# Linear attention and a gated MLP on one core: query features of the last two batches without the maximum, their two sums weighted afterwards, and a new order table

## The chip, the cores and the metric

The kernel runs on one core of a Trainium2 chip. The metric is the device time of one execution in microseconds (us). The time before is 264.87 us, the median of three runs that lie between 264.82 and 264.91 us.

The engines are named as the profile names them: PE (matrix products and transposes), PEld (its weight loads), DVE (vector), ACT (scalar, exponentials), POOL (GpSimd, which also issues the loads that change type) and SP (which issues most other transfers).

## The reference

There are 8 batches, 8 heads, 576 tokens, 64 numbers a head and 128 features. All inputs and the output are float32.

```python
def phi(x):
    proj = np.einsum('bhsd,df->bhsf', x, w_phi)
    proj = proj - np.max(np.abs(proj), axis=-1, keepdims=True)
    return np.concatenate([np.exp(proj), np.exp(-proj)], axis=-1)
q_p, k_p = phi(q), phi(k)
kv = einsum('bhsf,bhsd->bhfd', k_p, v);  z = sum(k_p, axis=2)
attn = (q_p @ kv) / (q_p . z + 1e-6)          # then heads side by side: x, 512 wide
h = max(x @ w_in, 0);  u, v = halves of h     # 1024 wide
v_n = (v - mean) / sqrt(var + 1e-6)
v_s = einsum('ts,bsd->btd', w_spatial, v_n) + b_spatial
out = (u * v_s) @ w_out
```

Each token and head has a maximum m over its projections p. The first half of its features is exp(p - m), the second exp(-p + m).

## The kernel before

**Tiling.** The 576 tokens of a batch are 4 blocks of 128 and a tail of 64. The tails of two batches make one tile, a group g (groups 0 to 3). Query work is cut into units (b, cc, hg): a batch, two of its four token blocks, four of its eight heads, so four units a batch, and one unit for each group of tails.

**A unit of queries before.** `qp` projects the queries with the tokens on the partitions (`by_token`, L578, 8 products of 64 rows). `qm` takes the largest absolute value over the features on DVE (`maxima`, L583). `qs` splits it on POOL into a high and a low bfloat16 part, mhl (`split`, L678 and L679). `qt` turns mhl on PE (`max_t`, L683), and `qc` copies it to mT (L277 on ACT or L279 on DVE). `qf` projects again with the features on the partitions and takes the maximum away inside the product: `features` issues 2 products with wphi (L689) and 8 with sel, a matrix of minus ones (L693). Two `qe` take the exponentials on ACT (L698), for p and for -p. `qn` (L748) sums over both halves of the features into one pair of PSUM banks, 16 products that accumulate in twos; column 64 of each head is the denominator. `qr` takes its reciprocal (L754) and `qx` multiplies (L759); both are on DVE and write x. The tails do the same with `qpt` to `qxt` (L799, L804, L809).

**Behind it.** The blocks of x are turned, by a DMA (`xx`) or on PE (`tx`, L824, copied by `txc`). `vm` and `um` are products with the halves of w_in (L853, L921), `vr` and `ur` their positive parts. `vb` and `va` are the moments on DVE (L875, L879), `vw` the root on POOL (L858 to L860), `vn` the normalised v on POOL (L863), `sm` the spatial product (L935, L937), `sg` the gate on DVE (L944), `om` the last product (L950), `oc` its copy, `od` its store. The second letter or a final t marks tails (`omt`, `sgt`).

**Keys.** `kp`, `km`, `ke` and `kem` make the key features; there the maximum is not subtracted. It goes as exp(-m) and exp(m) onto v instead: `vs` on POOL (L633), `vst` for tails (L645). `kv` is the sum over the tokens (L663, L665).

**What sets the order.** Nothing is scheduled by the program: ORDER is a table of words, and each word issues one step. `qn.7.0.0:2,3` is step qn of unit (7, 0, 0) with banks 2 and 3; `qx.7.0.0:0@V` runs on DVE (A is ACT, P is POOL, S is SP) into buffer 0 of its kind. Each engine works its own list in this order, and waits where an input or a buffer is not ready. `warm.5:3` issues 5 products of ident with itself that nobody reads (L365), into bank 3. BUFS gives the number of buffers of a kind.

**Loads.** Batch 0 of q and k is loaded as float32 by `lkf` and `lqf` from SP and ACT into buffers that are free at the start, and turned on PE as float32 (`turn`, L509). From batch 1 on, POOL issues loads that change the type to bfloat16 (`lk` L398, `lq` L402); these are turned on PE for batches 1 and, in part, 2, and by DMA later. Two steps for loading batch 1 as float32 (`lkg`, `lqg`) are in the program but not in the table.

**Ends.** The table ends with `om.6.3`, its copy on ACT and its store from SP. `omh`, `och` and `odh` do a block of the output in two halves of its columns.

Of the kernel before, what the change touches and what calls it, by code (L numbers as in the profile page):

```python
# [17 lines left out]
cident@P lkf.2:0@S lkf.1:4@A cident2@P warm.27:0 lkt.0:0@S lkf.0:1@A zsp@P zmhl.0@P lphi@S csel@P lqf.1:0@S zvst.0@P  # L18
lqf.0:1@S lkf.3:2@S tk.0.1.0:3 warm.3:0 chalf@P lv.0.0:3@S csel2@P warm.5:4 warm.3:0 lqt.0:1@S tkc.0.1.0:5@A lq.1:0@P
tk.0.0.0:2 warm.6:0 ctab@A lk.1:1@P tk.0.0.1:3 warm.12:0 tkc.0.0.0:0@V tkc.0.0.1@A cphi@V zvnt.0@P lvt.0:0@S  # L20
kp.0.0:4,5 kp.0.2:6,7 km.0.0:0@V warm.5:3 ke.0.2.1:0@A warm.5:2 warm.5:0 lv.0.1:1@S zmhl.3@P warm.5:2 ckt.0:0@P
ke.0.2.0@A warm.5:1 zmhl.2@P tkt.0:2 tq.0.1.0:3 kem.0.0:0@A km.0.2:1@V ke.0.0.0:1@A tq.0.1.1:1 warm.10:0 lkt.1:0@S
vsz.0.0:0@P zmhl.1@P tqc.0.1.0:6@A tktc.0:0@V kp.0.1:6,7 tqc.0.1.1@V warm.5:2 ke.0.1.0:2@A warm.5:0 warm.5:2 warm.5:0
ke.0.0.1@A km.0.1@V qp.0.0.1:2,3 warm.5:0 tq.0.0.1:1 qm.0.0.1:0@V kpt.0:4,5 warm.10:0 kem.0.1@A tqc.0.0.1:2@A
ke.0.1.1@A qp.0.1.1:0,1 lv.1.0:2@S qs.0.0.1:2@P tq.1.0.0:2 qm.0.1.1:1@V tq.0.0.0:3 kem.0.2:1@A tq.1.1.1:6 tqc.0.0.0@A
tk.0.1.1:7 tqc.1.0.0:1@V ket.0.0:0@A warm.5:0 qs.0.1.1:1@P tkc.0.1.1@V tq.1.1.0:3 warm.6:1 tqc.1.1.1:4@V vsz.0.1:1@A
qt.0.1.1:7 warm.5:2 ket.0.1@A tqc.1.1.0@V vs.0.1.1@P qt.0.0.1:6 qp.0.1.0:0,1 qc.0.0.1:0@V lbs:2@S kp.0.3:2,3
qm.0.1.0:2@V warm.5:6 qc.0.1.1:1@A vs.0.0.1@P ke.0.3.0:3@A warm.5:7 warm.5:6 kmt.0:0@V tq.1.0.1:6 ke.0.3.1@A
qs.0.1.0:2@P tk.1.1.0:7 lsp:0@P tk.1.1.1:0 tk.1.0.1:1 warm.4:4 tkc.1.1.1:3@A tkc.1.1.0@V lspt:3@P km.0.3@V
tkc.1.0.1:0@A lv.1.1:0@S qt.0.1.0:7 warm.5:4 lq.2:0@P cqt.0:0@A warm.5:4 kp.1.1:0,1 kemt.0:0@A vs.0.1.0@P tqc.1.0.1@A  # L30
tqt.0:5 km.1.1:2@V tk.1.0.0:4 tqtc.0:0@A warm.5:2 warm.4:3 lk.2:1@P tkc.1.0.0@A qpt.0:2,3 qc.0.1.0:3@V ke.1.1.0:4@A
# [135 lines left out]
def kernel(  # L167
# [900 lines left out]
```

## Time and profile before

| what | us |
| --- | --- |
| median of three runs | 264.87 |
| the profiled execution | 264.64 |
| its span, first to last instruction | 262.8 |
| outside the span | 1.84 |
| busy in the span: PE, DVE, ACT, POOL | 250.8, 206.6, 202.2, 185.1 |

A row of a timeline gives the start, the length and the engine, then the line, the operation, what is written and read, and a count of instructions that are alike. Products on PE overlap: one takes 0.2 to 0.4 us from its start to its end, but the next may start long before. What a row costs PE is therefore the distance from its start to the start of the next row. The busy sums count the fillers of `warm` too. Granted clock is the share of full speed that PE was given; it is 1.00 in every stretch of 10 us.

### The profile page before, as it was taken

The page shows a single profiled execution, that of the slowest core. Times are in us where ns is not written, and L with a number is a line of the kernel's source. Part 1 is how long each engine was busy: PE and PEld are TensorE (multiplying, and loading weights), DVE is VectorE, ACT ScalarE, POOL GpSimd, SP SyncE. Part 2 cuts the span into 40 slices and gives each one's busy share as a digit, 9 for nine tenths or more (in the row PEclk, how much of TensorE's full clock was granted, in tenths as well). Part 3 has the DMA queues.
Part 4 walks back from the last instruction along what each step waited for, and adds up shares of the span by engine and source line. Part 5 has one row for each costly group of instructions (what it writes and reads, how often), then busy time and mean ns, then how long its engine had stood idle before and what let it go on. Part 6 is the DMA issues. An engine that isn't in the chain of part 4 may idle for free.

```text
span 262.8 us, 8513 instructions
## 1 busy us (share of the span) xinstructions
PE 250.8 (95%) x3464; PEld 164.0 (62%) x3499; DVE 206.6 (79%) x362; ACT 202.2 (77%) x330; POOL 185.1 (70%) x338
## 2 busy tenths in 40 slices
PE   7999989999999998989999999999999999999993
PEld 7978768666566565666665766555547586446441
DVE  0679889998899898798899877999987848655730
ACT  3689989999769999999999896997899762453032
POOL 8627996999997996687999992369989820288000
PEclk9999999999999999999999999999999999999999
DMA  7999999962797979998999999998630130044045
GB/s 196 305 193 296 192 203 230 234 75 42 198 209 164 193 123 141 209 143 87 208 205 197 225 107 144 212 197 209 178 127 2 40 84 8 36 159 162 11 148 203
DMA packets 80090, 41.35 MB, mean 157 GB/s; under 512 B 48946, under 2 KB 75442, under 8 KB 80052
## 3 DMA queue, kind: packets, MB, share of 16 engines
q1 hardware_dynamic: 58628, 29.93, 53.1%
q0 software_dynamic: 20592, 10.10, 33.2%
q10 hardware_dynamic: 832, 0.79, 0.9%
q8 instruction: 27, 0.44, 0.7%
q14 instruction: 11, 0.09, 0.1%
HBM read 32.82 MB, written 9.44 MB: 161 GB/s over the span
## 4 chain that ended last, share of the span: by engine, by line
PE 67%; POOL 19%; DVE 5%; DMA 4%; issue 3%; ACT 0%; POOLq 0%; DVEq 0%; ACTq 0%
PE banks L853 10%; PE banks L950 9%; PE banks L935 9%; PE banks L921 8%; POOL vs L633 5%; PE banks L748 5%; PE banks L578 4%; PE banks L663 4%; DMA ld<-in_q_dram 4%; DVE mq L583 3%; PE banks L689 3%; POOL vn L863 2%; POOL vst L645 2%; PE banks L937 2%; PE banks L693 2%
## 5 line engine op out<-in xcount | busy, mean ns | idle before, releaser
L698 ACT ACTIVATE qf<-banks 128x1024 bf16<-128x1024 f32 x72 | 70.1, 1030 | 6.0 <-PE banks L693 5.5
L587 ACT ACTIVATE kf<-banks 128x1024 bf16<-128x1024 f32 x64 | 63.9, 1037 | 5.2 <-PE banks L578 4.8
L633 POOL TENSOR_TENSOR vs<-v,em 128x512 bf16<-128x512 f32 x64 | 65.7, 1043 | 3.0 <-ACT em L592 2.8
L583 DVE TENSOR_REDUCE mq<-banks 128x8 f32<-128x1024 f32 x36 | 43.4, 1220 | 4.1 <-PE banks L578 2.5
L583 DVE TENSOR_REDUCE mk<-banks 128x8 f32<-128x1024 f32 x32 | 38.8, 1218 | 4.5 <-ACT kf L587 2.4
L921 PE MATMUL banks<-xT,w_u 128*128 128x512 bf16 x128 | 32.3, 380 | 0.0
L935 PE MATMUL banks<-w_spT,vn 128*128 128x512 bf16 x116 | 31.6, 379 | 0.7 <-issue 0.2
L853 PE MATMUL banks<-w_v,xT 128*128 128x512 bf16 x118 | 31.2, 379 | 0.5
L950 PE MATMUL banks<-w_out,uT 128*128 128x512 bf16 x113 | 29.6, 379 | 0.7 <-issue 0.2
L277 ACT COPY ob<-banks 128x512 f32<-128x512 f32 x23 | 13.5, 597 | 19.4 <-PE banks L950 18.7
L944 DVE TENSOR_TENSOR uT<-banks,uT 128x512 bf16<-128x512 f32 x32 | 21.4, 683 | 6.4 <-PE banks L937 6.1
L863 POOL TENSOR_SCALAR vn<-vr,mv,rs 128x512 bf16<-128x512 bf16 x32 | 24.4, 767 | 1.2
L663 PEld LDWEIGHTS <-kf 128*128 128x128 bf16 x512 | 21.9, 97 | 4.3 <-issue 0.8
L663 PE MATMUL banks<-vs,kf 128*128 128x66 bf16 x512 | 23.9, 194 | 0.5 <-POOL vs L633 0.3
L875 DVE BATCH_NORM_STATS2 st<-vr 128x6 f32<-128x512 bf16 x32 | 21.5, 683 | 3.5 <-ACT vr L283 3.2
L578 PE MATMUL banks<-wphi,T 64*128 64x128 bf16 x512 | 22.8, 217 | 0.4
L759 DVE TENSOR_TENSOR x<-banks,rc 128x512 bf16<-128x512 f32 x32 | 22.1, 690 | 0.9
L283 ACT ACTIVATE vr<-banks 128x512 bf16<-128x512 f32 (+1 forms) x28 | 16.8, 606 | 7.3 <-PE banks L853 5.8
L748 PEld LDWEIGHTS <-qf 128*128 128x128 bf16 x512 | 19.2, 98 | 4.4 <-issue 0.9
L365 PE MATMUL banks<-ident 128*128 128x128 bf16 x237 | 19.4, 234 | 2.1 <-POOL ident L279 1.7
L665 PE MATMUL banks<-vst,kft 128*128 128x66 bf16 x128 | 21.1, 191 | 0.1
L748 PE MATMUL banks<-kv,qf 128*128 128x66 bf16 x512 | 21.0, 193 | 0.0
(123 smaller groups left out, 481.2 us busy)
## 6 DMA issues: line engine op xcount, KB each, us to landing
v<-in_v_dram SPq DMA_DIRECT2D x16, 512.0 KB, 6.9
out_dram<-ob SPq DMA_DIRECT2D x31, 256.0 KB, 3.0
ld<-in_q_dram POOLq DMA_DIRECT2D x7, 512.0 KB, 10.8
ld<-in_k_dram POOLq DMA_DIRECT2D x7, 512.0 KB, 10.4
uT<-in_q_dram SPq DMA_DIRECT2D x2, 512.0 KB, 5.3
vt<-in_v_dram SPq DMA_DIRECT2D x8, 128.0 KB, 8.6
out_dram<-ob SPq DMA_DIRECT2D x8, 128.0 KB, 3.3
vn<-in_moe_w_spatial_dram POOLq DMA_DIRECT2D x1, 576.0 KB, 7.8
```

Source lines behind the costliest of these rows:

```text
L578: nc.tensor.matmul(out=bank(banks[y])[:, n * F:(n + 1) * F], lhsT=xT[halves[y], n, :], rhs=wphi[halves[y], :], start=True, stop=True)
L583: nc.vector.tensor_reduce(out=out_, in_=pp.rearrange("p y (n f) -> p y n f", f=F), axis=AX.X, op=ALU.max, apply_absolute_value=True)
L587: nc.scalar.activation(out=kf[:, s].rearrange("p y n f -> p y (n f)"), in_=pp, func=AF.Exp, bias=0.0, scale=(1.0, -1.0)[s])
L633: ENG[e].tensor_tensor(out=get("vs", (b, j))[:, s, :, 0:D], in0=at["v", (b, j // 2)][:, (j % 2) * n:(j % 2 + 1) * n, :], in1=at["em", (b, ...
L663: nc.tensor.matmul(out=pv[:, hh, s, :], lhsT=kf[:, s, c % 2, 2 * hh + c // 2, :], rhs=w[:, s, NB * hh + c, :], start=(c == 0), stop=False)
L698: nc.scalar.activation(out=at["qf", u][:, s].rearrange("p y n t -> p y (n t)"), in_=at["pq", u], func=AF.Exp, bias=0.0, scale=(1.0, -1.0)[s])
L748: nc.tensor.matmul(out=at["pn", u][:, y, n, :], lhsT=f[:, s, y, n, :], rhs=at["kv", b][:, hg * HH + n, s, :], start=(s == 0), stop=(s == 1))
L853: nc.tensor.matmul(out=bank(place)[r], lhsT=lhs[:, kc, r], rhs=w_v[:, kc, :], start=(kc == 0), stop=(kc == KC - 1))
L863: ENG[e].tensor_scalar(out=out_, in0=in_, scalar1=mv, scalar2=rs, op0=ALU.add, op1=ALU.mult)
L921: nc.tensor.matmul(out=bank(place).rearrange("p (c t) -> p c t", c=NB), lhsT=w_u[:, kc, dc * P:(dc + 1) * P], rhs=at["xT", b][:, :, kc, :] ...
L935: nc.tensor.matmul(out=bank(place), lhsT=at["vn", b][:, c, cs], rhs=w_spT[:, c, 0:T0], start=(c == 0), stop=False)
L950: nc.tensor.matmul(out=bank(place), lhsT=at["uT", b][:, dc, c * P:(c + 1) * P], rhs=w_out[:, dc, :], start=(dc == 0), stop=(dc == KC - 1))
```

## The change

The units of batches 6 and 7 and the tail unit of group 3 no longer subtract the maximum from the query projections, in the way the keys do already. With f1 = exp(p) and f2 = exp(-p), the result is (exp(-m) f1.kv1 + exp(m) f2.kv2) divided by the same of z. It may be multiplied above and below by exp(-m), so only the first sum needs a weight, w = exp(-2m).

- `qw` (ACT) makes w from the maximum; `qs`, `qt` and `qc` go.
- `qg` is the projection alone, the 2 products with wphi; the 8 with sel go.
- `qn` becomes `qna` and `qnb`, 8 products each, for the two halves of the features, each into its own pair of banks.
- `qy` (DVE) writes w times the first sum to tq, 528 float32 numbers a partition; `qz` (DVE) adds the second sum; `qv` (DVE) takes the reciprocal of the denominators. `qu` multiplies tq by it into x and runs on POOL. `qr` and `qx` go.
- tq has one buffer, wq has six. The float32 copy of w_phi now lies in a buffer of x.

The table is new from its first word. Beside these steps it loads batch 1 of q and k by `lkg` and `lqg` (float32, issued by SP) and no longer by POOL; the 8 turnings of batch 1 are float32 with it. Ahead of the last product stand 195 fillers in place of 232, and behind it 10 in place of 5. It ends with `om.7.2` and the second half of `omh.7.3`. Many copies and positive parts go to another engine of ACT and DVE than before.

```diff
-BUFS = dict(ld=3, ..., mq=4, mhl=4, mT=4,
+BUFS = dict(ld=3, ..., mq=4, mhl=4, mT=4, wq=6, tq=1,
...
+        wq=([P, 2, HH], FP32),
+        tq=([P, 2, HH, DA], FP32),
...
-    wphi_f = const("wphi_f", [D, F], FP32)
+    wphi_f = buf["x"][0][0:D].rearrange("p a h d -> p (a h d)").bitcast(FP32)[:, 0:F]
...
+    def features_u(u, xT):
+        banks = [places.pop(0), places.pop(0)]
+        for y in range(2):
+            nc.tensor.matmul(out=bank(banks[y]).rearrange("p (n t) -> p n t", n=HH), lhsT=wphi[halves[y], :],
+                             rhs=xT[halves[y]], start=True, stop=True)
+        at["pq", u] = pair(*banks)
+
+    def weight(u):
+        nc.scalar.activation(out=get("wq", u), in_=at["mq", u], func=AF.Exp, bias=0.0, scale=-2.0)
...
+    def half_sums(b, cc, hg, s):
+        u = (b, cc, hg)
+        f = at["qf", u]
+        pn = at["pn", u, s] = sums((places.pop(0), places.pop(0)))
+        for y in range(2):
+            for n in range(HH):
+                nc.tensor.matmul(out=pn[:, y, n, :], lhsT=f[:, s, y, n, :], rhs=at["kv", b][:, hg * HH + n, s, :],
+                                 start=True, stop=True)
...
+    def weigh(u, w, r=slice(0, P)):
+        nc.vector.tensor_tensor(out=get("tq", u)[r], in0=at["pn", u, 0][r],
+                                in1=at["wq", w][r].unsqueeze(3).to_broadcast([r.stop - r.start, 2, HH, DA]), op=ALU.mult)
+
+    def join(u, r=slice(0, P)):
+        t = at["tq", u][r]
+        nc.vector.tensor_tensor(out=t, in0=at["pn", u, 1][r], in1=t, op=ALU.add)
+
+    def inverse(u, r=slice(0, P)):
+        nc.vector.reciprocal(out=get("rc", u)[r], in_=at["tq", u][r, :, :, D:D + 1])
+
+    def divide(e, out_, u, r=slice(0, P)):
+        ENG[e].tensor_tensor(out=out_, in0=at["tq", u][r, :, :, 0:D],
+                             in1=at["rc", u][r].to_broadcast([r.stop - r.start, 2, HH, D]), op=ALU.mult)
```

The tails do the same by `qwt`, `qgt`, `qnat`, `qnbt`, `qyt`, `qzt`, `qvt`, `qut`. One line of the old table and one of the new, both from the end of batch 7:

```diff
-qn.7.1.1:4,5 qx.7.0.0:1@V vr.6.3:0@A txt.3.2:2 um.6.3:3 qr.7.1.1:1@V sg.5.1@V qx.7.1.1:2@V vm.6.0:1 txtc.3.2:0@V
+qz.7.1.1@V tx.7.1:1 txc.7.0:0@A om.5.0:7 qv.7.1.1:2@V vb.6.1:3@V qu.7.1.1:2@P umt.3:0 txc.7.1@V vb.6.3:1@V
```

Three places show what moves. The first is PE in batch 7. Before, from the last subtraction of one unit through the next unit's two products with wphi to its first subtraction:

```order
L693 LDWEIGHTS sel
L693 MATMUL banks<-mT_114,sel 128x128
L689 LDWEIGHTS wphi
L689 MATMUL banks<-T_68,wphi 128x512
L689 LDWEIGHTS wphi
L689 MATMUL banks<-T_68,wphi 128x512
L693 LDWEIGHTS sel
L693 MATMUL banks<-mT_113,sel 128x128
```

After, the projection of unit (7, 1, 0), between the second sums of two other units (L703 is the product of `features_u`, L789 that of `half_sums`):

```order
L789 LDWEIGHTS qf_127
L789 MATMUL banks<-kv_102,qf_127 128x66
L703 LDWEIGHTS wphi
L703 MATMUL banks<-T_68,wphi 128x512
L703 LDWEIGHTS wphi
L703 MATMUL banks<-T_68,wphi 128x512
L789 LDWEIGHTS qf_126
L789 MATMUL banks<-kv_103,qf_126 128x66
```

The projection stands alone; the subtractions that followed it are gone, and other units' sums stand around it.

The second place is DVE at the last two units of batch 7, whose results are turned on PE next. Before, each is a reciprocal and a product straight into x:

```order
L754 RECIPROCAL rc_122<-banks 128x8
L759 TENSOR_TENSOR x_127<-banks,rc_122 128x2x256
L754 RECIPROCAL rc_124<-banks 128x8
L759 TENSOR_TENSOR x_126<-banks,rc_124 128x2x256
L875 BN_STATS st_139<-vr_134 128x6
```

After (L801 weighs, L806 adds, L809 inverts; L985 and L989 are the moments of batch 6, L282 copies):

```order
L801 TENSOR_TENSOR tq_123<-banks,wq_117 128x528
L989 BN_AGGR mv_154<-st_146 128x2
L806 TENSOR_TENSOR tq_123<-banks,tq_123 128x528
L809 RECIPROCAL rc_131<-tq_123 128x8
L985 BN_STATS st_149<-vr_141 128x6
L282 COPY xT_136<-banks 128x512
L985 BN_STATS st_147<-vr_144 128x6
L989 BN_AGGR mv_153<-st_147 128x2
L801 TENSOR_TENSOR tq_123<-banks,wq_121 128x528
L989 BN_AGGR mv_154<-st_149 128x2
L806 TENSOR_TENSOR tq_123<-banks,tq_123 128x528
L809 RECIPROCAL rc_129<-tq_123 128x8
```

Each unit has three DVE steps instead of two, x is no longer written by DVE, and the moments of batch 6 stand between the units. Both units write the one buffer tq_123.

The third place is POOL at the same units. Before, no unit's result passes POOL; there stand only the moments' root and the normalisation of batch 6 (L858 to L863):

```order
L858 TENSOR_SCALAR mv_144<-mv_144 128x2
L859 TENSOR_SCALAR mv_144<-mv_144 128x2
L860 TENSOR_TENSOR rs_150<-mv_144,neghalf 128x2
L863 TENSOR_SCALAR vn_154<-vr_138,mv_144,rs_150 128x512
L858 TENSOR_SCALAR mv_143<-mv_143 128x2
```

After, the division of the last two units (L812) stands ahead of and behind that work (L968 to L973):

```order
L812 TENSOR_TENSOR x_134<-tq_123,rc_131 128x2x256
L968 TENSOR_SCALAR mv_154<-mv_154 128x2
L969 TENSOR_SCALAR mv_154<-mv_154 128x2
L970 TENSOR_TENSOR rs_160<-mv_154,neghalf 128x2
L973 TENSOR_SCALAR vn_163<-vr_143,mv_154,rs_160 128x512
L812 TENSOR_TENSOR x_134<-tq_123,rc_129 128x2x256
L968 TENSOR_SCALAR mv_153<-mv_153 128x2
```

The last unit's division waits on POOL behind a root and a normalisation, and the next weighing on DVE may write tq only when the division before it has read it.

More of the change, by code (lines that the diff above doesn't have):

```diff
@@ L28 @@
[L28 to L31, printed above, removed]
-warm.5:6 qmt.0:3@V warm.5:5 vstz.0:0@P qp.0.0.0:6,7 vst.0.0.1@P qf.0.1.0:4,5 ke.1.1.1@A lqt.1:1@S qm.0.0.0:0@V
@@ L159 @@
+od.6.3@S om.7.0:3 oc.7.1:3@A od.7.1@S omh.7.3.0:0 oc.7.0:2@V om.7.2:2 och.7.3.0:0@A od.7.0@S odh.7.3.0@A omh.7.3.1
+oc.7.2:4@V warm.5:7 och.7.3.1@A warm.5:5 od.7.2@S odh.7.3.1@A
 """
-BUFS = dict(ld=3, T=7, v=4, tl=1, tf=2, tT=1, vt=1, kf=5, kft=1, mk=4, mkt=1, em=4, emt=1, vs=4, vst=1, kv=3, mq=4, mhl=4, mT=4,
+BUFS = dict(ld=3, T=7, v=4, tl=1, tf=2, tT=1, vt=1, kf=5, kft=1, mk=4, mkt=1, em=4, emt=1, vs=4, vst=1, kv=3, mq=4, mhl=4, mT=4, wq=6, tq=1,
             qf=5, rc=3, x=3, xt=1, xT=3, xTt=2, vr=5, st=4, mv=6, rs=5, vn=3, vnt=2, uT=3, uTt=2, ob=5)
```

330 lines of the change are left out of this document (195 added, 135 removed).

## Prediction

> **What bounds the kernel now.** I read the page first, then the stretches of 10 us, then the chain that ended last, then PE's timeline near the end. The page gives each engine's busy time:
>
> ```profile
> PE 250.8 (95%) x3464; PEld 164.0 (62%) x3499; DVE 206.6 (79%) x362; ACT 202.2 (77%) x330; POOL 185.1 (70%) x338
> ...
> PE 67%; POOL 19%; DVE 5%; DMA 4%; issue 3%; ACT 0%; POOLq 0%; DVEq 0%; ACTq 0%
> ```
>
> The second row is the share of each engine in the chain. PE holds two thirds of it, and POOL a fifth. Where, the stretches say (start:end, length, then busy time of PE, PEld, DVE, ACT and POOL with their counts, granted clock, DMA share, GB/s):
>
> ```profile
> 100.00:110.00 10.00, 9.26 (x147) 6.26 (x146) 7.89 (x16) 9.34 (x14) 5.36 (x8) 1.00 1.29 194
> 110.00:120.00 10.00, 8.98 (x155) 6.10 (x155) 9.46 (x17) 8.94 (x18) 8.65 (x17) 1.00 1.00 139
> ...
> 210.00:220.00 10.00, 9.79 (x211) 7.54 (x212) 5.56 (x14) 5.94 (x11) 1.57 (x2) 1.00 0.26 56
> 182.00:215.00 33.00, 32.58 (x509) 20.92 (x515) 26.10 (x48) 26.78 (x44) 27.04 (x49) 1.00 0.32 92
> ```
>
> Between 100 and 120 us PE stands for 0.74 + 1.02 = 1.76 us. From 182 us on it has next to no idle time (0.42 of 33 us), while DVE falls to 5.56 and POOL to 1.57 of 10 us. The edited units lie in this last regime: there a product less on PE is time won, and work added to DVE and POOL has room. The head, in which PE waits for loads and is fed with fillers, has rows of its own below.
>
> **What the nine units lose on PE.** Rows of PE's timeline; the distance between starts is the cost:
>
> ```profile
> 205.39 0.38 PE L689 MATMUL banks<-T,wphi 64*128 64x512 bf16 x2
> 205.60 0.39 PE L693 MATMUL banks<-mT,sel 64*128 64x128 bf16 x8
> 205.83 0.38 PE L689 MATMUL banks<-T,wphi 64*128 64x512 bf16 x2
> 206.04 0.39 PE L693 MATMUL banks<-mT,sel 64*128 64x128 bf16 x8
> 206.36 1.04 PE L1017 MATMUL banks<-w_out,uTt 128*128 128x512 bf16 x4
> ...
> 208.31 0.67 PE L748 MATMUL banks<-kv,qf 128*128 128x66 bf16 x16
> 208.83 0.27 PE L683 MATMUL banks<-ident,mhl 128*128 128x128 bf16 x2
> 208.94 1.03 PE L935 MATMUL banks<-w_spT,vn 128*128 128x512 bf16 x3
> ```
>
> The 8 subtractions take 205.83 - 205.60 = 0.23 us, and 2.07 over eight units and one tail. A turn of the maximum takes half of 208.94 - 208.83, 0.055 us, so 0.50 over nine. Together **-2.57 us**, all on the path by the rows above. The sums stay 16 products (0.52 us), only in two banks more. Going from products of 64 rows to 128 costs 206.36 - 206.04 - 0.23 = 0.09 us more; the new table has 53 runs of 64-row work where the old had 55. At 0.09 us out and, by estimate, as much in, that is 0.2 to 0.4: **-0.3**.
>
> **The head.** The table's fillers ahead of the last product go from 232 to 195. Batch 1 is turned as float32. The rows of fillers, of float32 turnings and of a bfloat16 one between them:
>
> ```profile
> 7.09 0.50 PE L365 MATMUL banks<-ident 128*128 128x128 bf16 x6
> 7.43 0.61 PE L509 MATMUL banks<-ident_f,ob 128*128 128x128 f32 x4
> 7.87 0.83 PE L365 MATMUL banks<-ident 128*128 128x128 bf16 x12
> ...
> 17.30 0.40 PE L509 MATMUL banks<-ident,ld 128*128 128x128 bf16 x4 [0.60 <-DMA ld<-in_q_dram]
> 17.54 0.61 PE L509 MATMUL banks<-ident_f,uT 128*128 128x128 f32 x4
> ```
>
> A filler takes (7.43 - 7.09)/6 = 0.057 us, so 37 fewer are 2.1 us. They are not work but cover for waits; taking them out wins only what the waits themselves lose. A float32 turning takes 7.87 - 7.43 = 0.44 against 17.54 - 17.30 = 0.24, so eight cost 0.20 each, 1.6 us, in a part where PE has room. If the waits shrink as the fillers do, the head is worth 1.6 - 2.1 = **-0.5 us**. Bounds: nothing of the fillers comes back (+1.6, float32 turnings exposed) and all of it with the turnings hidden (-2.1). I take the middle since PE's work in the head is about the fillers that go.
>
> The Trainium skill (FP8 and Floating Point Precision, TensorE Precision Notes) says that true FP32 makes four passes through the array. The trace does not bear that out for these turnings: 0.44 against 0.24 is not two passes. What four would do stands among the rivals.
>
> What makes this possible is how the loads stand:
>
> ```profile
> 6.50 10.76 DMA ld<-in_q_dram
> ...
> ld<-in_q_dram POOLq DMA_DIRECT2D x7, 512.0 KB, 10.8
> ...
> uT<-in_q_dram SPq DMA_DIRECT2D x2, 512.0 KB, 5.3
> ...
> 3.37 1.14 SPq L386 DMA_DIRECT2D uT<-in_q_dram  x2
> ```
>
> Batch 1's queries sit on the chain for 10.76 us. Issued by SP as float32, loads of that kind landed after 5.3 us, not 10.8. SP pays 1.14/2 = 0.57 us an issue, 2.3 us for four, and the loads of v and of the tails behind them start that much later.
>
> **What DVE, ACT and POOL gain.** Groups that do what the new steps do (count, busy time, mean ns of one):
>
> ```profile
> L759 DVE TENSOR_TENSOR x<-banks,rc 128x512 bf16<-128x512 f32 x32 | 22.1, 690 | 0.9
> L944 DVE TENSOR_TENSOR uT<-banks,uT 128x512 bf16<-128x512 f32 x32 | 21.4, 683 | 6.4 <-PE banks L937 6.1
> L279 DVE COPY ob<-banks 128x512 f32<-128x512 f32 x12 | 8.1, 677 | 0.1
> L633 POOL TENSOR_TENSOR vs<-v,em 128x512 bf16<-128x512 f32 x64 | 65.7, 1043 | 3.0 <-ACT em L592 2.8
> L863 POOL TENSOR_SCALAR vn<-vr,mv,rs 128x512 bf16<-128x512 bf16 x32 | 24.4, 767 | 1.2
> L860 POOL TENSOR_TENSOR rs<-mv,neghalf 128x2 f32<-128x2 f32 x16 | 11.2, 699 | 0.0
> L754 DVE RECIPROCAL rc<-banks 128x8 f32<-128x8 f32 x32 | 6.5, 203 | 5.2 <-PE banks L748 3.1 <-PE banks L683 1.4 <-PE banks L365 0.4
> L592 ACT ACTIVATE em<-mk 128x8 f32<-128x8 f32 x8 | 1.2, 206 | 0.4 <-DVE mk L583 0.4
> 227.84 0.19 POOL L858 TENSOR_SCALAR mv<-mv 128x2 f32<-128x2 f32 x1 [16.27 <-DVE mv L879]
> ```
>
> Weighing and adding read PSUM and one SBUF tile; the nearest rows are 690 and 683 ns, and writing float32 costs nothing extra (677 for the copy to ob). For 528 in place of 512 numbers I take 0.71 us each; bounds are 0.68 and, if the float32 operand from SBUF is as dear as on POOL, 1.04. DVE gains 9 x (2 x 0.71 - 0.69) = 6.6 us less some copies of mT. POOL's division is nearest to vs, float32 by a broadcast into bfloat16: 1.04 us, 9.4 in all, less the splits; the 16.27 us for which POOL stood idle before 227.84 are about where it goes. The weight is 0.21 us on ACT. None of it is on the path by load.
>
> By latency it can be. A unit is now weigh, add, invert, divide, 0.71 + 0.71 + 0.20 + 1.04 = 2.66 us, where reciprocal and product took 0.89; and tq has one buffer, so DVE may not weigh the next unit before POOL has divided this one. I walked the new order by these durations against PE's work between. Two places are tight. At `tx.7.0` the tail's division (POOL) holds tq, the unit's weighing starts after it, and x comes some 0.4 to 0.5 us after PE is ready. At `tx.7.2` the last division stands on POOL behind a root (0.19 + 0.19 + 0.70) and a normalisation (0.77), and x comes about when PE does: 0 to 0.5. For both I take **+0.8 us**.
>
> **The end.** Rows of the last copy, and the stores by queue:
>
> ```profile
> 257.62 0.59 ACT L277 COPY ob<-banks 128x512 f32<-128x512 f32 x1 [0.66 <-PE banks L950]
> 258.21 0.44 PE L365 MATMUL banks<-ident 128*128 128x128 bf16 x5
> 258.45 0.59 ACT L277 COPY ob<-banks 128x512 f32<-128x512 f32 x1 [0.25 <-PE banks L950]
> out_dram<-ob SPq DMA_DIRECT2D x31, 256.0 KB, 3.0
> out_dram<-ob ACTq DMA_DIRECT2D x2, 128.0 KB, 2.5
> ```
>
> The last block becomes half a block: its copy is shorter and its store lands 0.5 us sooner, but a whole block's copy on DVE (0.68) starts only one half product (0.44) ahead of it. I take **-0.3**. The ten fillers behind the last product are beside the copies.
>
> **Sum.** -2.57 - 0.3 - 0.5 - 0.3 + 0.8 = -2.9 us. The profiled execution took 264.64, so 261.8; the median stands 0.23 above that execution, so **262.0 us**. A measurement of this kernel tells 0.2% (0.5 us) from no change.
>
> **The rivals.** *The ring through tq sets the pace (slower).* From the first half sum to the last turning the new order gives PE 33.5 us of work, by distances between starts such as those above. DVE has in the same stretch 9 x (2 x 0.71 + 0.20) = 14.6 us of weighing, adding and inverting; by its list, fourteen gates, copies, positive parts and moments of about 0.68 and some 3.6 us of smaller steps, 13.1 together. If it also stood still for every division (9.4) and for two hand-overs a unit (18 of about 0.1), it would need 38.9: 5.4 us more than PE, so -3.7 + 5.4 = +1.7, **266.6 us**. It decides when less than about 1.1 us of other DVE work stands between one unit's inversion and the next weighing. For it: the one buffer. Against it: in most gaps the list has two gates, or moments and a copy (1.3 us and more), and before DVE had 6.9 us free in 182 to 215 us. At 1.04 us for weighing and adding it would be the same story, 6 us more DVE work. I give it 0.14.
>
> *POOL in the middle.* The first and the last of the longer pieces of the chain's stretch on POOL:
>
> ```profile
> 117.48 1.00 POOL vs L633
> ...
> 151.27 2.01 POOL vs L633 x2
> ```
>
> POOL led from 117 to 153 us, and 19% of the chain are 50 us. The new table has the same `vs` and `vst`, puts three small casts more on POOL and takes two loads away. If they are placed worse by 1.5 to 3 us, of the size of the 1.76 us of 100 to 120, the time is 263.5 to 265: 0.12.
>
> *The head gives it back.* The four loads on SP hold up v and the tails by 2.3 us and all of it is seen: 264.3 us, 0.08. *Float32 in four passes.* At 4 x 0.24 = 0.96 us a turning, eight would add 5.8 us, 4.2 more than counted, and with no waits in the head to hide them the time is 266.2; the 0.44 of the trace leaves that 0.01.
>
> **How the numbers follow.** The forecast has 0.65, by itself from 259.8 (no waits at the tight places, -0.8; half of the 1.76 us gone, -0.9; the head better by 0.5) to 263.5 (the tight places 0.5 dearer, the head worse by 1.0). Faster by over 0.2%: 0.65, 0.03 of POOL and 0.02 of the head, 0.70. Within: 0.05 of POOL and 0.04 of the head, 0.09. Slower: 0.14 of the ring, 0.04 of POOL, 0.02 of the head and the 0.01 of four passes, 0.21. The range is 259.8 to 266.0: it leaves out the upper part of the ring and of the four passes, and what is better than the forecast's own lower end.
>
> **What would show it.** Right: the new products at L703 take about 0.22 us and nothing follows them; PE is without idle time after 180 us but for up to a microsecond ahead of the turnings of batch 7; weighing and adding take 0.70 to 0.72 and the division 1.04; the first long run of idle-free PE starts no later than before. Wrong: PE's idle time names DVE tq or POOL x in several units (the ring), POOL heads the chain for more than 50 us (the middle), or loads end PE's waits beyond 20 us (the head).

## The result, and the profile after

The changed kernel takes **260.55 us** in the median of four runs (260.25 to 261.82), the kernel before, run beside it, 264.89 (264.82 to 264.93). The ratio is 0.9846 with an interval of 0.9813 to 0.9878. A second measurement gave 260.78 (260.63 to 261.65) against 264.62, a ratio of 0.9862 (0.9848 to 0.9877). The forecast was 262.0 in a range of 259.8 to 266.0: the sign and the range held, and the gain was 4.3 us where 2.9 were forecast. The profiled execution took 260.25, its span 258.5, against 264.64 and 262.8; it is the fastest of its four. Four single executions of the kernels below took 4 to 9 us longer than the fastest of their kernel; they are left out of all medians and ratios.

Busy time and chain of the page after:

```profile
PE 250.4 (97%) x3386; PEld 160.1 (62%) x3386; DVE 214.2 (83%) x362; ACT 201.2 (78%) x335; POOL 190.6 (74%) x331
...
PE 65%; DVE 12%; POOL 11%; ACT 5%; issue 3%; DMA 1%; POOLq 0%; DVEq 0%; ACTq 0%
```

PE is as long busy as before (250.8) in a span that is 4.3 us shorter; POOL's share of the chain fell from 19% to 11%, the loads' from 4% to 1%.

Four stretches of before (start:end, length, busy time and counts of PE, PEld, DVE, ACT and POOL, clock, DMA share, GB/s), then the same stretches and 100 to 120 us of after:

```profile
0.00:50.00 50.00, 46.08 (x771) 38.85 (x773) 36.90 (x57) 39.83 (x69) 37.99 (x72) 1.00 1.19 233
50.00:180.00 130.00, 126.82 (x1841) 80.05 (x1861) 115.89 (x203) 117.41 (x189) 105.55 (x190) 1.00 1.11 165
180.00:215.00 35.00, 34.52 (x539) 22.04 (x545) 28.10 (x51) 28.56 (x46) 28.87 (x53) 1.00 0.35 95
215.00:250.00 35.00, 34.79 (x275) 18.68 (x278) 23.48 (x50) 12.32 (x21) 12.63 (x25) 1.00 0.24 78
```

```profile
0.00:50.00 50.00, 47.28 (x764) 39.07 (x765) 40.41 (x59) 40.35 (x73) 40.37 (x75) 1.00 1.11 245
50.00:180.00 130.00, 128.91 (x1875) 79.61 (x1874) 121.06 (x206) 117.45 (x189) 106.73 (x191) 1.00 1.05 175
180.00:215.00 35.00, 34.90 (x458) 20.46 (x455) 28.98 (x50) 28.59 (x50) 26.69 (x38) 1.00 0.34 106
215.00:250.00 35.00, 35.00 (x273) 18.45 (x269) 22.07 (x48) 12.92 (x23) 16.84 (x29) 1.00 0.20 62
...
100.00:110.00 10.00, 9.96 (x163) 6.43 (x162) 9.60 (x13) 9.86 (x15) 7.67 (x14) 1.00 1.14 162
110.00:120.00 10.00, 10.00 (x179) 6.61 (x176) 9.77 (x20) 9.74 (x18) 9.46 (x16) 1.00 1.27 148
```

PE's idle time between 50 and 180 us falls from 3.18 to 1.09 us, and the 1.76 us of 100 to 120 are 0.04 now. From 180 us on there is 0.10 where there was 0.69. With PE full to that degree, what is left to compare is what PE does, and for that busy time is too coarse, since products overlap. So I took the distance from the start of each step's first product to the start of the next step's, and set it against the shortest such distance for a step of its kind; what is above is a wait. Worked out so over all of PE's steps:

| part of the difference, us | before | after | difference |
| --- | --- | --- | --- |
| to 50 us: fillers | 12.21 | 10.72 | -1.49 |
| to 50 us: waits | 7.28 | 5.70 | -1.58 |
| to 50 us: turnings of batch 1 as float32, and changes between 64 and 128 rows | 3.45 | 3.26 + 1.76 | +1.57 |
| 50 to 180 us: waits and a run of fillers | 5.17 | 4.01 | -1.16 |
| 50 to 180 us: changes between 64 and 128 rows | 6.03 | 5.84 | -0.19 |
| the nine units | | | -2.5 |
| from 180 us to the last product: waits | 0.1 | 0.8 | +0.75 |
| from the last product to the end of the span | 4.59 | 4.91 | +0.3 |
| sum | | | -4.3 |

One part of the waits to 50 us is set by no order. PE works at half speed at the start of every profiled run. In the view of the windows the granted clock reads 1.00 there too, but the distances of the fillers tell it. Eleven fillers and the turning behind them, in the profiled run of after and in that of the last kernel below, whose table is the same up to there (its lines are five higher):

```profile
5.34 0.78 PE L368 MATMUL banks<-ident 128*128 128x128 bf16 x11
5.96 0.61 PE L512 MATMUL banks<-ident_f,ob 128*128 128x128 f32 x4
```

```profile
6.06 1.38 PE L373 MATMUL banks<-ident 128*128 128x128 bf16 x11
7.23 0.85 PE L517 MATMUL banks<-ident_f,ob 128*128 128x128 f32 x4
```

They take 0.62 us in the first, 0.056 each, and 1.17 us in the second, 0.106 each. The traces record from when on full clock was granted: 4.55 us here, 7.73 us there, 6.72 us in the profiled run before. So (6.72 - 4.55)/2 = 1.1 of the 1.58 us by which the waits of the head fall is an earlier clock in this one execution. In the second profiled run of the changed kernel (6.16 us) everything from 7 us on stands 0.77 us later, and the head gains 0.7 instead of 1.5. The last section has the other runs.

The groups that the change made, by line:

```profile
L801 DVE TENSOR_TENSOR tq<-banks,wq 128x528 f32<-128x528 f32 x9 | 6.3, 698 | 2.5 <-PE banks L789 2.0 <-POOL x L812 0.3
L806 DVE TENSOR_TENSOR tq<-banks,tq 128x528 f32<-128x528 f32 x9 | 6.4, 706 | 1.4 <-PE banks L789 0.8
L809 DVE RECIPROCAL rc<-tq 128x8 f32<-128x8 f32 x9 | 1.8, 201 | 0.2
L812 POOL TENSOR_TENSOR x<-tq,rc 128x512 bf16<-128x512 f32 x8 | 8.4, 1046 | 10.3 <-DVE rc L809 7.2 <-issue 3.1
L708 ACT ACTIVATE wq<-mq 128x8 f32<-128x8 f32 x9 | 1.9, 215 | 0.0
```

All five came as forecast (0.71, 0.71, 0.20, 1.04 and 0.21). In the last column of L801 stands the ring: DVE waited 0.3 us for POOL to give tq back, in all nine units together. The 10.3 us in the row of L812 are idle time of POOL, which costs nothing where x still comes in time.

At the two places that the forecast called tight, rows of after around the turnings of batch 7:

```profile
218.54 1.04 POOL L812 TENSOR_TENSOR x<-tq,rc 128x512 bf16<-128x512 f32 x1 [2.13 <-DVE rc L809]
219.33 0.41 PE L789 MATMUL banks<-kv,qf 128*128 128x66 bf16 x8
219.64 0.40 PE L934 MATMUL banks<-ident,x 128*128 128x128 bf16 x4
...
226.56 1.04 POOL L812 TENSOR_TENSOR x<-tq,rc 128x512 bf16<-128x512 f32 x1
227.66 0.57 PEld L934 LDWEIGHTS <-x 128*128 128x128 bf16 x8 [0.19 <-POOL x L812]
227.80 0.61 PE L934 MATMUL banks<-ident,x 128*128 128x128 bf16 x8
```

At `tx.7.0` x is ready at 218.54 + 1.04 = 219.58, and the turning starts at 219.64, 0.07 us behind the half sums (0.24 us from 219.33). At `tx.7.2` x is ready at 227.60 and the weights are loaded at once; PE itself has work until 227.80. Both are just in time. The 0.75 us stand elsewhere:

```profile
182.72 1.03 PE L963 MATMUL banks<-w_v,xT 128*128 128x512 bf16 x4
183.59 1.89 PE L1031 MATMUL banks<-xT,w_u 128*128 128x512 bf16 x8
185.31 1.29 PE L1045 MATMUL banks<-w_spT,vn 128*128 128x512 bf16 x4
```

Four products of this size take 1.03 us; the spatial product of `sm.4.3` takes 1.29. The other 0.5 are pieces of at most 0.1 us between 187 and 225.

The end of after:

```profile
253.16 0.60 PE L1079 MATMUL banks<-w_out,uT 128*128 128x256 bf16 x4
253.41 0.69 DVE L282 COPY ob<-banks 128x512 f32<-128x512 f32 x1 [0.66 <-PE banks L1060]
253.59 0.72 PE L368 MATMUL banks<-ident 128*128 128x128 bf16 x10
253.79 0.37 ACT L280 COPY ob<-banks 128x256 f32<-128x256 f32 x1 [0.88 <-PE banks L1079]
254.20 0.36 ACTq L1091 DMA_DIRECT2D out_dram<-ob  x1
```

PE is done with its last product at 253.59 where that was 258.21, so 4.6 us are gone by then. The last copy ends at 253.79 + 0.37 = 254.16, and 4.3 us are left to the end of the span at 258.5. Before, it was 3.8 us, from 258.45 + 0.59 = 259.04 to 262.8. Time from issue to landing of the last store of after, and of that of a later kernel (the second order under "The end") that has no whole block's store beside it:

```profile
out_dram<-ob ACTq DMA_DIRECT2D x1, 128.0 KB, 2.6
```

```profile
out_dram<-ob ACTq DMA_DIRECT2D x1, 128.0 KB, 1.9
```

Before, the last store, a whole block, took 2.5 us. So half the bytes did not make it shorter here, where the store of a whole block was issued 0.07 us ahead of it; alone it does. The rest of the span stands behind the landing: 262.8 - 259.07 - 2.5 = 1.2 us before, 258.5 - 254.20 - 2.6 = 1.7 us after. What sets that rest no run shows.

### The profile page after: what moved, and what is told of

Same layout as the page of the kernel before. It is cut to its first block, busy times and chain, and to the rows that moved or that the text cites. A ratio compares the mean times of both kernels' runs of the same rounds, so it can differ in the third digit from the quotient of the medians.

```text
span 258.5 us, 8359 instructions
## 1 busy us (share of the span) xinstructions
PE 250.4 (97%) x3386; PEld 160.1 (62%) x3386; DVE 214.2 (83%) x362; ACT 201.2 (78%) x335; POOL 190.6 (74%) x331
## 4 chain that ended last, share of the span: by engine, by line
PE 65%; DVE 12%; POOL 11%; ACT 5%; issue 3%; DMA 1%; POOLq 0%; DVEq 0%; ACTq 0%
PE banks L1045 9%; PE banks L963 7%; PE banks L1060 7%; PE banks L1031 5%; PE banks L581 5%; PE banks L666 5%; PE banks L368 4%; POOL vn L973 4%; ACT kf L590 3%; PE banks L761 3%; POOL vs L636 3%; PE banks L1047 2%; PE banks L512 2%; DVE mk L586 2%; PE banks L692 2%
## 5 line engine op out<-in xcount | busy, mean ns | idle before, releaser
L590 ACT ACTIVATE kf<-banks 128x1024 bf16<-128x1024 f32 x64 | 62.9, 1031 | 3.1 <-PE banks L581 1.7
L1045 PE MATMUL banks<-w_spT,vn 128*128 128x512 bf16 x128 | 33.5, 380 | 0.3
L963 PE MATMUL banks<-w_v,xT 128*128 128x512 bf16 x128 | 32.0, 380 | 0.0
L1060 PE MATMUL banks<-w_out,uT 128*128 128x512 bf16 x124 | 30.7, 379 | 0.0
L973 POOL TENSOR_SCALAR vn<-vr,mv,rs 128x512 bf16<-128x512 bf16 x32 | 24.5, 772 | 1.1
L286 ACT ACTIVATE vr<-banks 128x512 bf16<-128x512 f32 (+1 forms) x26 | 15.5, 602 | 11.3 <-PE banks L963 10.2
L280 ACT COPY ob<-banks 128x512 f32<-128x512 f32 (+1 forms) x22 | 12.5, 568 | 14.1 <-PE banks L1060 11.9
L985 DVE BATCH_NORM_STATS2 st<-vr 128x6 f32<-128x512 bf16 x32 | 21.4, 679 | 1.8 <-ACT vr L286 1.7
L581 PEld LDWEIGHTS <-T 64*128 64x128 bf16 x512 | 16.0, 94 | 8.0 <-issue 4.8
L648 POOL TENSOR_TENSOR vst<-vt,emt 64x512 bf16<-64x512 f32 x16 | 16.6, 1041 | 5.0 <-ACT emt L595 4.3
L1031 PEld LDWEIGHTS <-w_u 128*128 128x128 bf16 x128 | 11.7, 97 | 13.0 <-issue 0.8
L1045 PEld LDWEIGHTS <-vn 128*128 128x128 bf16 x128 | 11.1, 97 | 12.7 <-POOL vn L973 1.9
## 6 DMA issues: line engine op xcount, KB each, us to landing
ld<-in_q_dram POOLq DMA_DIRECT2D x6, 512.0 KB, 10.3
```

Source lines behind the costliest of these rows:

```text
L581: nc.tensor.matmul(out=bank(banks[y])[:, n * F:(n + 1) * F], lhsT=xT[halves[y], n, :], rhs=wphi[halves[y], :], start=True, stop=True)
L590: nc.scalar.activation(out=kf[:, s].rearrange("p y n f -> p y (n f)"), in_=pp, func=AF.Exp, bias=0.0, scale=(1.0, -1.0)[s])
L963: nc.tensor.matmul(out=bank(place)[r], lhsT=lhs[:, kc, r], rhs=w_v[:, kc, :], start=(kc == 0), stop=(kc == KC - 1))
L973: ENG[e].tensor_scalar(out=out_, in0=in_, scalar1=mv, scalar2=rs, op0=ALU.add, op1=ALU.mult)
L985: nc.vector.bn_stats(out=get("st", (b, c)), in_=at["vr", (b, c)])
L1031: nc.tensor.matmul(out=bank(place).rearrange("p (c t) -> p c t", c=NB), lhsT=w_u[:, kc, dc * P:(dc + 1) * P], rhs=at["xT", b][:, :, kc, :] ...
```

## The experiments

Nine kernels are edits of the changed kernel, one is an edit of the kernel before, and one puts the new arithmetic into the old table; none leaves out any of the computation. "After" below is the changed kernel. It was also run once more as it is, whose result stands above:

> The changed kernel once more, beside the others of this set, so that they have a time of the same chip to stand against. Every theory expects 260.3 to 260.9 us, 0.982 to 0.986 of the kernel before.

 In the rows of the experiments the lines are two to five higher than in after where the program grew.

**The subtraction put back.** The 8 products of a unit return, with zeros in place of the maximum, so that they cost and change nothing:

```diff
-                             rhs=xT[halves[y]], start=True, stop=True)
+                             rhs=xT[halves[y]], start=True, stop=False)
+        for n in range(HH):
+            for y in range(2):
+                nc.tensor.matmul(out=bank(banks[y])[:, n * P:(n + 1) * P], lhsT=sel[halves[y], n, :],
+                                 rhs=nought[halves[y], :], start=False, stop=(n == HH - 1))
```

> The changed kernel with the 8 subtracting products of each of the nine units back on PE, fed with zeros (a tile set to zero at the start), so that nothing waits for the maximum and the result is the same. Theory (PE bounds the late stretch, so the products taken off PE were time): 9 x 0.23 = 2.07 us slower than the changed kernel, about 262.6 us, and the time of the last product later by as much. Rival (the ring through the one buffer tq, DVE and POOL set the pace of the late stretch, PE had room): less than 0.5 us slower, about 260.8 us, with idle time of PE filled.

Measured: 262.51 us (262.13 to 263.45), 0.9926 of before (0.9913 to 0.9939), 1.7 to 2.0 above after, by its two medians. By the starts of steps that both kernels have, 0.59 us of the profiled run lie ahead of 180 us, where nothing differs (the later clock, see the last section); the units add 1.56, of 9 x 0.23 = 2.07. Three quarters of the products' time come back in the time of the kernel. Of the other 0.5 us, the waits behind 180 us, counted as above, give 0.36, and the products themselves come to 1.9 and not 2.07 by the distances of this run. The step of the forecast that carries the change holds.

**Batch 1 by POOL again.** After with the old kind of load:

```diff
-lkg.1:2@S ... lkg.0:0@S ... lqg.0:0@S ... lqg.1:1@S
+lk.1:1@P ... lq.1:2@P
```

> The changed kernel with batch 1 of q and k loaded by POOL as bfloat16 again, at the places in the table where SP issued the float32 loads; the eight turnings are bfloat16 with it (1.6 us less on PE). Theory (the head gained 1.5 us because these loads land sooner from SP): slower by 1 to 3 us, 261.5 to 263.5 us, with PE idle in the first 30 us waiting for the loads. Rival (the loads are hidden either way and the head's gain is that of the order of its steps): within 0.5 us, or faster by up to 1.6 us, 259.0 to 261.0 us.

Measured: 263.04 us (262.28 to 264.34), 0.9936 (0.9916 to 0.9955): 2.3 to 2.5 above after, and all of it is there by 26 us. The POOL rows, of after and then of this kernel, with what PE does behind the second:

```profile
13.74 4.05 POOL L636 TENSOR_TENSOR vs<-v,em 128x512 bf16<-128x512 f32 x4
18.31 0.20 POOL L681 CAST mhl<-mq 128x8 bf16<-128x8 f32 x1
```

```profile
4.42 1.14 POOL L404 DMA_DIRECT2D ld<-in_k_dram  x1
5.57 0.89 POOL L408 DMA_DIRECT2D ld<-in_q_dram  x1
16.64 4.05 POOL L639 TENSOR_TENSOR vs<-v,em 128x512 bf16<-128x512 f32 x4 [2.76 <-DMA v<-in_v_dram]
21.21 0.19 POOL L684 CAST mhl<-mq 128x8 bf16<-128x8 f32 x1
...
22.72 0.23 PE L689 MATMUL banks<-ident,mhl 128*128 128x128 bf16 x1 [1.32 <-POOL mhl L685]
```

It is not the loaded batch that is late. The two loads of POOL are in flight beside the load of v, which SP has issued. In after that load is issued at 5.15 us and takes 7.4 us, here at 5.26 and takes 11.2. v lands so late that POOL waits 2.76 us for it, the four `vs` start 2.9 us later, the splits of the maxima stand behind them on POOL, and PE waits for a split. POOL's own time for the two issues, 2 us, costs nothing, since it then stands idle for 3.64 us more. This run had its full clock late, at 7.70 us, and at 8 us stands 1.5 us behind after; the wait for the split takes that in, since POOL sets its end. In the kernel with both costs put back (below) full clock came at 5.32 us, and yet PE gets the split at 22.84, 0.12 us later than here, after 1.60 us of waiting. The 2.3 to 2.5 us are the price of POOL's loads at this place of the table: they start at 4.42 us. The old table starts them at 6.50 and 7.65, behind the load of v at 5.26; the new table with that order was not tried.

**Batch 1 by SP in the old table.** The kernel before with the new kind of load, words in place of words:

```diff
-lq.1:0@P ... lk.1:1@P
+lqg.0:0@S lqg.1:1@S ... lkg.1:2@S lkg.0:1@S
```

> The kernel before with batch 1 of q and k loaded by SP as float32, at the places in its table where POOL issued the loads; nothing else is changed, so the eight turnings are float32 (1.6 us more on PE). Theory (sooner landings let the head run ahead): 263.4 to 264.7 us. Rival (the old order of the head does not use them and pays for the turnings): 265 to 266.5 us.

Measured: 265.43 us (265.18 to 266.25), 1.0027 (1.0018 to 1.0035): slower than before by 0.7. The last product starts 0.05 us later than before's; the rest lies behind it, as the span shows (263.3 against 262.8): 1.7 us stand behind the landing of the last store where the kernel before has 1.2, and no run shows why. The loads alone are worth nothing: the old table has `vs` on POOL only from 18.5 us on, behind the splits, with and without them, and v takes 6.9 us from issue to landing in both, so v is not awaited. The rival was right.

**Both put back.** After with the zeros and with POOL's loads:

> The changed kernel with both costs put back at once: the eight products of a unit that the change took off PE (with zeros as the weights, so the values stay) and batch 1 loaded by POOL's queue in bf16 as before. Alone the first gave 262.5 and the second 263.0 where the changed kernel gives 260.6. Theory (the gain is these two things plus a smaller rest in the middle and in the turn): they add, 264.4 to 265.0, within 0.2% of the time before. Rival (the new order of the middle gains by itself, whatever the loads and the units cost, and the two additions share the same slack): clearly below, 263.0 to 263.8.

Measured: 264.55 us (263.42 to 265.28), 0.9984 of before (0.9969 to 0.9999). The two costs add: 1.7 to 2.0 and 2.3 to 2.5 on after's 260.6 to 260.8 are 264.8 to 265.1. So products and loads carry the gain, and the rest of the change together comes to about -0.2 us, by the interval between 0 and -0.8. From the table above that rest is the middle (-1.35), the turn (-0.5), the late waits and the end (+1.05), and a head that with POOL's loads is 2.4 - 1.5 = 0.9 us slower in the new order than in the old: +0.1. The head's part is rough, since it rests on single executions: the profiled run here stands 3.8 us behind after at 25 us, 1.0 of it because 19 fillers behind the wait for the split ran at half speed (granted clock 0.50 from 22.4 to 25.8 us).

**A second tq.** Another buffer for the ring, in a view of a load buffer that is free by then; every second unit uses it:

```diff
+    buf["tq"].append(buf["ld"][0].rearrange("p h x -> p (h x)").bitcast(FP32)[:, 0:2 * HH * DA]
+                     .rearrange("p (y n d) -> p y n d", y=2, n=HH))
...
-qy.6.1.1:0@V ... qy.6.0.1:0@V ... qyt.3.2:0@V ... qy.7.1.1:0@V
+qy.6.1.1:1@V ... qy.6.0.1:1@V ... qyt.3.2:1@V ... qy.7.1.1:1@V
```

> The changed kernel with two buffers of tq taken in turn (the second lies in a buffer of ld that is no longer read by then), so that DVE can weigh the next unit while POOL divides the last one. Theory (the ring is covered by other work): within 0.3 us of the changed kernel, 260.2 to 260.8 us. Rival (the ring sets the pace): faster by 1 us or more, under 259.6 us, with the waits of the weighing for POOL gone.

Measured: 260.49 us (260.17 to 261.17), 0.9846 (0.9834 to 0.9859): no difference. The single buffer does not set the pace, as the 0.3 us in the row of L801 say.

**The division on DVE.** `qu` and `qut` go from POOL to DVE, at the same places of the table:

```diff
-qu.6.1.0:0@P ... qu.7.1.0@P
+qu.6.1.0:0@V ... qu.7.1.0@V
```

> The changed kernel with the division of the nine units done by DVE in place of POOL. DVE then has nine more operations of about 0.7 us, POOL nine of 1.05 us fewer. Theory (PE alone bounds the kernel from 100 us on, and what DVE and POOL do behind a unit is covered): 260.3 to 261.5. Rival (DVE, busy 0.97 of the time from 100 to 140 us, is a second bound there, so that its work shows one for one): five of the nine units fall there or before, 262.5 to 265.

Measured: 263.29 us (262.85 to 263.90), 0.9948 (0.9935 to 0.9960): 2.5 to 2.7 slower than after. My theory fell; the rival has the size, but the place that I gave it was wrong, since all nine units are divided after 195 us. By the starts of common steps the profiled run has 1.3 us ahead of 10 us, which is the later clock (last section), and adds 2.35 between 203 and 222 us. Rows there:

```profile
202.51 2.04 POOL L639 TENSOR_TENSOR vs<-v,em 128x512 bf16<-128x512 f32 x2
203.67 1.42 DVE L815 TENSOR_TENSOR x<-tq,rc 128x512 bf16<-128x512 f32 x1
205.02 0.68 DVE L285 COPY ob<-banks 128x512 f32<-128x512 f32 x1
205.75 1.05 PE L1101 MATMUL banks<-xTt,w_u 128*128 128x128 bf16 x16 [0.95 <-DVE ob L285]
...
224.35 0.64 PE L792 MATMUL banks<-kv,qf 128*128 128x66 bf16 x16 [0.54 <-DVE tq L804]
```

What DVE does late, PE waits for: a copy that clears a bank (0.95), a weighing that clears one (0.54). DVE has idle time in after, but not at these places. And one division took 1.42 us where seven others took 0.67 to 0.70: it ran beside two `vs` of POOL and ended half a microsecond after them. The Trainium skill (SBUF — State Buffer, Who interferes with whom) says that a DVE instruction with two SBUF inputs contends with a GpSimd instruction that reads SBUF, through a lock that is exclusive. This row agrees; it is one row, and no kernel here tried that alone.

**New arithmetic, old table.** The steps of the new arithmetic written into the old table at the places of the old ones; weight for turn and copy, and the two half sums of a unit one behind the other in the same pair of banks, so that the second waits for the weighing of the first. The diff at one unit:

```diff
-qn.6.1.1:6,7 ... qr.6.1.1:1@V ... qx.6.1.1:2@V
+qna.6.1.1:6,7 ... qy.6.1.1:0@V ... qnb.6.1.1:6,7 qz.6.1.1@V qv.6.1.1:1@V qu.6.1.1:2@P
```

> The new steps of the nine units in the old table: the splits, turns and copies are taken out, the weight stands where the copy stood, the first half sum where the sum stood, the weighing where the reciprocal stood, and second half sum, adding, inverting and dividing where the product stood, in the banks of the old sum. Loads, fillers and all else are as before. Theory (PE bounds the late stretch and the arithmetic alone is worth its 2.57 us of PE less what this placing by hand adds in waits): 262.4 to 264.0 us. Rival (the gain is the new table's, the arithmetic by itself only moves waits to DVE and POOL): 264.9 us or slower.

Measured: 280.97 us (279.99 to 281.02), 1.0608 (1.0595 to 1.0622): 16 us slower than before. My theory fell. PE's waits after 180 us, and stretches of 10 us:

```profile
PE banks L791 <- DVE tq L803: 9.6, 6, 2.0
```

```profile
200.00:210.00 10.00, 7.05 (x102) 4.19 (x99) 7.37 (x14) 6.04 (x10) 7.29 (x10) 1.00 0.01 2
210.00:220.00 10.00, 8.04 (x142) 5.92 (x141) 4.91 (x10) 4.46 (x11) 5.51 (x6) 0.83 0.17 39
220.00:230.00 10.00, 6.04 (x85) 3.56 (x84) 5.58 (x11) 3.32 (x5) 3.00 (x3) 1.00 0.20 43
230.00:240.00 10.00, 7.04 (x46) 4.05 (x46) 5.57 (x11) 0.58 (x1) 2.21 (x3) 0.66 0.07 27
```

PE stands before second half sums for DVE's weighing, 9.6 us in six waits, and no engine is full at 200 to 240 us: this is a chain of short hand-overs, sum, weigh, sum, add, invert, divide, turn, that the old order leaves bare. The granted clock falls too, to 0.83 and 0.66 of full speed. So the arithmetic saved its 2.5 us in the order that puts other work between its steps and gives each half sum banks of its own, and not in this hand-made placing. Which of the two counts for how much was not tried.

**No fillers in the head.** After without its 195 fillers ahead of the last product:

```diff
-warm.5:1 warm.1:0 ... warm.11:6 ... warm.4:3
```

> The changed kernel without the 195 fillers ahead of the last product. Theory (they stand in waits only, and taking them out moves no work): within 0.5 us of the changed kernel, 260.0 to 261.0 us, with PE idle where they stood and the granted clock unchanged at 1.00. Rival (PE's clock or its first products after a wait suffer when it stands still): slower by 1 us or more, with the products of the head taking longer or a granted clock below 1.00.

Measured: 261.07 us (260.23 to 261.56), 0.9850 (0.9835 to 0.9864): 0.3 to 0.5 above after. The granted clock (the last column but two) did drop:

```profile
14.20:17.60 3.40, 3.23 (x33) 2.89 (x33) 2.96 (x3) 2.70 (x4) 3.40 (x4) 0.51 1.20 306
17.60:24.50 6.90, 4.67 (x58) 3.58 (x57) 6.42 (x9) 6.69 (x14) 6.65 (x18) 0.99 1.17 299
24.50:31.30 6.80, 6.54 (x93) 4.96 (x91) 5.35 (x8) 3.77 (x11) 5.23 (x15) 0.50 1.18 217
```

Half speed for 10.2 us and yet 0.3 to 0.5 us lost by the medians; the profiled run, the slowest of its four, is 1.3 us longer than that of after. The time that most fillers take is time that PE waits in any case, and most of the work at half speed fits into it. So taking 27 of them out of the head can hardly have won much by itself; that the loads and the order shortened the waits is what remains, argued and not tried alone.

**The end.** Three orders. The first puts `om.7.2` ahead of both halves of the last block:

```diff
-omh.7.3.0:0 oc.7.0:2@V om.7.2:2 och.7.3.0:0@A od.7.0@S odh.7.3.0@A omh.7.3.1 oc.7.2:4@V warm.5:7 och.7.3.1@A warm.5:5 od.7.2@S
+om.7.2:2 oc.7.0:2@V od.7.0@S omh.7.3.0:0 oc.7.2:4@A od.7.2@S omh.7.3.1 och.7.3.0:0@V odh.7.3.0@A warm.5:7 och.7.3.1@A warm.5:5
```

> The changed kernel with the whole block om.7.2 ahead of both halves of om.7.3 at the end of the table, its copy on ACT and the first half's on DVE, so that the last store of a whole block starts about 0.7 us sooner. Theory (the end of 4.9 us after the last product is set by the store of that whole block): 0.3 to 0.6 us faster, 259.9 to 260.3 us. Rival (the end is a fixed cost behind the last store, whichever it is): within 0.15 us of the changed kernel.

Measured: 261.47 us (260.73 to 261.69), 0.9871 (0.9858 to 0.9883), no gain. Of the 1.3 us by which its profiled run is longer than that of after, 1.2 are there at 10 us (the later clock). The last copy on ACT waited 1.24 us, which the trace lays to the ten fillers that stood before it on PE. The second has no fillers there and puts `och.7.3.0` ahead of `omh.7.3.1`:

```diff
-oc.7.2:4@A od.7.2@S omh.7.3.1 och.7.3.0:0@V odh.7.3.0@A warm.5:7 och.7.3.1@A warm.5:5
+oc.7.2:4@A od.7.2@S och.7.3.0:0@V odh.7.3.0@A omh.7.3.1 och.7.3.1@A
```

> The changed kernel with another order after the last unit: the third output product stands ahead of both halves of the last one, its copy on ACT and the first half's copy on DVE follow at once, and the fillers behind the last product are gone. Theory (the 4.9 us from the last product to the end are the last copy, which waits for an engine that still does the copy before it, and the last transfer): 0.3 to 0.7 us less than the changed kernel, 259.9 to 260.3. Rival (the last transfer alone sets the end, and the copies are covered): no difference, 260.5 to 260.8.

Measured: 260.55 us (260.31 to 260.87), 0.9841 (0.9828 to 0.9854): as after. The rival has the number, not the reason. Its end:

```profile
254.00 0.42 DVE L285 COPY ob<-banks 128x256 f32<-128x256 f32 x1 [0.66 <-PE banks L1082]
254.48 0.60 PE L1082 MATMUL banks<-w_out,uT 128*128 128x256 bf16 x4 [0.57 <-DVE ob L285]
255.11 0.37 ACT L283 COPY ob<-banks 128x256 f32<-128x256 f32 x1 [0.97 <-PE banks L1082]
```

The second half product writes the bank that the first one's copy still reads, and waits 0.57 us for it; after had `om.7.2` in that gap. What the end wins (the last store lands 1.9 us after its issue, not 2.6), the last product loses. The third has this end and the second tq:

> The order of e10_end and a second buffer for the weighed numerators, so that the next unit's weighing does not wait for the division of the one before. Theory (each was worth 0 to 0.5 us alone and they touch different places): 259.6 to 260.2, the fastest of the kernels tried. Rival (the buffer is worth nothing and the end was not the last copy's wait): 260.4 to 260.8, as the changed kernel.

Measured: 261.18 us (260.26 to 261.81), 0.9854 (0.9837 to 0.9871). Its profiled run is 1.57 us longer than that of after, and 1.52 of it are there at 10 us. No version beats the changed kernel by more than its runs differ among themselves.

## Why the prediction came out as it did, step by step

- **What bounds it** was right: PE, from 182 us on without idle time, so that a product less is time won. The zeros put back show it.
- **Units**, -2.57 forecast, -2.5 by the starts. Right, and the larger part (the subtraction, 2.07 taken, 1.9 by the distances) shown by the first experiment.
- **Runs of 64 rows**, -0.3: by the starts -0.19 in the head and -0.19 in the middle. Right, not tested apart.
- **The head**, -0.5 taken, -1.5 by the starts in the profiled run and -0.7 in the second one, inside the bounds of -2.1 and +1.6. This term was mis-sized. The step that failed reads "If the waits shrink as the fillers do": only 27 of the 37 fillers stood in the head (-1.49), the turnings cost 1.76, and the waits fell by 1.58 as well, of which 1.1 is the earlier clock of that execution, a thing that no term of the sum had. The mechanism was half seen. The forecast had the landing of batch 1 as the point and feared that v would come later behind SP's four issues ("the head gives it back"). v was hardly held up: it takes 7.4 us from its issue at 5.15, before 6.9 us from 5.26. It was the other loads that could hold it up, as the second experiment shows. `vs` starts at 13.74 us, before at 18.54, because the new order has it ahead of the splits; the third experiment shows that the loads without that order win nothing.
- **The middle** was put at nothing in the sum, with only a rival to the slow side; it is the larger miss that both profiled runs show. The 1.76 us of 100 to 120 us, quoted in the forecast's first part, were won back; 1.35 us over 50 to 180. Why the new order does better there was not isolated.
- **The tight places**, +0.8 for `tx.7.0` and `tx.7.2`: 0.07 us at the first and none at the second, where x is there 0.2 us before PE is. Waits of 0.75 us stand at other places. The size agrees by chance.
- **The end**, -0.3 forecast, +0.3 measured. The step that failed took half the bytes for 0.5 us less of transfer: the last store took 2.6 us beside that of a whole block, and 1.9 only where that one was out of the way. The rest is the stretch behind the landing, 1.2 us before and 1.7 after, which the sum did not have. With batch 1 by SP in the old table, whose end is that of before, it was 1.7 too, so it differs without a cause in the order.
- **The rivals.** The ring through tq had 0.14; the second buffer changed nothing. Where it would have come from, DVE as a second bound, the division on DVE shows: 2.35 us. POOL in the middle went the other way. Four passes for float32 did not show: the eight turnings cost 1.76 us more than bfloat16 ones, 0.22 each where 0.20 was taken. A turning takes 0.44 and a bfloat16 one 0.22 by the shortest distances, so twice as long; the forecast's "not two passes" came from a row of 0.24.

The forecast's 2.9 us fall short of 4.3 by the middle (1.16) and the head (0.8), both without the runs of 64 rows, less the end (0.6). The head's share is that of the fastest of four executions; in the second profiled run there is next to nothing of it, and the gain of the medians there is 264.62 - 260.78 = 3.8.

## What to carry to other kernels

Where one engine is full, count its instructions: that part of the gain was forecast to a tenth of a microsecond here. But an edit that cuts work and lengthens a chain is worth its count only in an order made for it; the same arithmetic, put by hand into the old one, cost 16 us, so read the table with the arithmetic, not after it. And at the start of a kernel ask of each load what it delays, not only what it brings: in the new table POOL's loads of batch 1 matter by holding up v. Before a single execution is taken apart, find out when PE got its full clock.

## What the runs showed of the hardware

- Without fillers the granted clock halves in pieces of 3.4 us (14.2 to 17.6) and 6.8 us (24.5 to 31.3) and returns. In the 3.4 us ahead of the first piece PE was busy for 1.85 us, ahead of the second for 1.62; the 3.4 us before those, with 2.98, kept full clock. The Trainium skill (TensorE: Matmul & The Clock Gate, Part 1) describes a gate with a window of about 3.4 us and half rate; the rows agree. What I had not expected is that these ten microseconds of half speed cost only 0.3 to 0.5 us by the medians.
- At the start the same half speed costs its full price in the new table. The changed kernel's four runs spread over 1.6 us (260.25 to 261.82), before's beside them over 0.1. The traces of eight kernels with the new table and SP's loads tell what divides them, the moment from which full clock is granted:

| profiled run | full clock from, us | behind after at 10 us, us |
| --- | --- | --- |
| after | 4.55 | 0 |
| a second tq | 5.01 | 0.22 |
| the end, second order | 6.00 | 0.69 |
| the subtraction put back | 6.02 | 0.70 |
| after once more | 6.16 | 0.77 |
| the end, first order | 7.08 | 1.21 |
| the division on DVE | 7.14 | 1.24 |
| the end, and a second tq | 7.73 | 1.52 |

The lag is half of the clock's delay, within 0.1 us in each, and up to 25 us it stays as it is. The delays span 3.2 us, so this alone gives a spread of 1.6 us. What PE does up to there is the same in all eight, so none of the edits sets the moment. That the kernel before, whose profiled run had full clock at 6.72 us, spreads so little may be because it waits for loads behind that; this was not tried. A profiled run of such a kernel is compared by its stretches, not by its total.
